# Second attention of a two-layer convolution/attention kernel: P*V by whole token halves, output rows begun with two quarters, the maximum of two quarters subtracted on TensorE, stores inside the written order

## The chip, the cores and the metric

One core of a Trainium2 chip runs the whole program. The metric is the device time of one execution in microseconds (us), lower is better. The engines are called PE (TensorE), DVE (VectorE), ACT (ScalarE), POOL (GpSimd) and SP (SyncE, which here only issues DMA transfers).

## The reference, cut to what matters

The input `x` is [1, 2048, 512]. Two layers follow each other, and both have a long convolution (part A) and a sliding attention with dilation (part B), each behind a layer norm and with a residual:

```
x = x + A(layernorm(x))     # y = irfft(rfft(K) * rfft(u)) + u * Dskip
x = x + B(layernorm(x))
x = x + A(layernorm(x))
x = x + B(layernorm(x))     # "the second attention": the part that is changed

def B(x):                   # 32 heads of 16; window of 8 keys, 2 apart
    q, k, v = split(x @ wqkv)
    logits[s, w] = q[s] . k[s - 2 w] / 4      (masked where s - 2 w < 0)
    attn = softmax(logits over w)
    o[s] = sum over w of attn[s, w] * v[s - 2 w]
    return o @ wo
```

## The kernel before

The 2,048 tokens lie as 16 rows `j` of 128 tokens; four rows form a group `X0` to `X3` (`Xg`). The 512 features are worked in four quarters `i` of 128 (8 heads each), the 16 rows in two token halves `jh` of 8 rows. For each quarter and half, `b_layer` does the following steps.

- `K` and `Q` (`proj`, L1170, L1173): PE projects, ACT copies out of PSUM. `V` (`proj_v`, L1257, L1264), then `M` (`v_shift`, L1281): DMAs on SP and POOL copy shifted rows of the value table.
- `L` (`logits`, L1218/L1220 and L1242): DVE multiplies queries with shifted keys, PE sums over the features of a head, ACT copies the logits to `Lsb`.
- `S` (`softmax`): DVE takes the maximum (L1301, L1307, L1309, with one PE exchange between the two lane halves). Then either DVE subtracts it in place (L1312) and ACT takes the exponent (L1313), which is what the second attention does; or, with `pe_max`, PE subtracts it in PSUM by two 512-column matmuls (L1319, L1320) and ACT takes the exponent from there (L1322), which is what the first attention does. PE sums the exponents (L1327), ACT takes the reciprocal (L1329, L1330), DVE multiplies (L1331).
- `P` (`pv_part`): DVE multiplies probabilities with shifted values (L1352), PE folds the products (L1362), ACT copies them out to `oT` (L1373). A part covers `nj` rows, 8 or 4, by the table `pv`. With 8 rows, one DVE instruction of 128x2048 does both lane halves of a key pair; with 4 rows two of 128x512 are issued.
- `R` (`out_row`): one output row `j`, 128 tokens by 512. PE adds up the residual (identity matmul, L1387) and four terms, one for each quarter of `oT` (L1389, the last one L1392 in rows of `early` and `early_l`). ACT or DVE copies the row out (L1406, L1404). For rows in `added`, the identity matmul is left out and DVE adds the residual as it copies (L1408). A row in `early` or `early_l` is begun when three quarters are there, and its last term is a step of its own.

The steps of one attention are put in order by a string that is written out in the source (`order` in `LAYERS`): every word is one step, `S31j` for instance step `j` of the softmax of quarter 3, half 1, and a `+` behind a word picks the second of its possible engines. Each engine runs its steps in the order of that string. The class `Plan` checks the order and keeps a running time from its own table of costs, from which alone it decides how many filler matmuls on zeros `stream` puts in PE's gaps (L1085); `keep=(share, columns)` says how much of a gap may be filled and how many columns are wanted in 3.41 us. In the order, `P28` is the part of quarter 2 from row 8, `P2c` that from row 12; rows 8 to f are hexadecimal.

After the last step, `store_x` issues seven stores: group 0 whole, group 1 whole, the rows of group 2 singly, group 3 whole, alternately on SP and on ACT:

```
for g in range(NG):
    n = 1 if g in LATE_GROUPS else 4
    for k in range(0, 4, n):
        (nc.sync if (g + k) % 2 == 0 else nc.scalar).dma_start(ov[...], Xg[g][:, k:k + n, :])
```

Of the kernel before, what the change touches and what calls it, by code (L numbers as in the profile page):

```python
# [11 lines left out]
ACT = mybir.ActivationFunctionType  # L12
# [8 lines left out]
D = 512  # L21
# [123 lines left out]


def store_x(nc, Xg, out2d):
    ov = out2d.rearrange("(p j) d -> p j d", j=NJ)
    for g in range(NG):
        n = 1 if g in LATE_GROUPS else 4  # L150
        for k in range(0, 4, n):
            (nc.sync if (g + k) % 2 == 0 else nc.scalar).dma_start(ov[:, g * 4 + k:g * 4 + k + n, :], Xg[g][:, k:k + n, :])
# [699 lines left out]
class Plan:  # L852
# [44 lines left out]
    def run(self, order):  # L897
# [16 lines left out]
        if todo:  # L914
# [9 lines left out]
LATE_GROUPS = (2,)  # L924
# [33 lines left out]
         pe_max=True,  # L958
# [3 lines left out]
         keep=(0.7, 4500),  # L962
# [4 lines left out]
         whole=()),  # L967
    dict(order="y0a y0b n0a n0b n0c y0c y0d n0d n0e n0i n0h y1a y1b y1c y1d n0f n1a n1c n0g n1b n1e n1d y2a n0j y2b y2c y3a n2a n0k n0l n1i n1g "
# [22 lines left out]
               "P3cj Reb Rcb R8a Rdb Rec Rcc+ Raa Rbb Rdc Rfa Rfb R8b Rab R9b",  # L991
         pv=[[8, 8], [8, 8], [8, 4], [8, 4]],
         soft=[0, 0, 0, 0],
         pe_max=False,
         early=[6, 12],
         early_l=[1, 4, 13, 14],
# [616 lines left out]
```

## Time and profile before

| | us |
|---|---|
| median of 3 runs | 438.28 (436.13 to 438.46) |
| profiled execution | 439.68 |
| span in its profile | 437.9 |
| DVE busy in the span | 402.4 (92%) |
| PE busy in the span | 379.9 (87%) |
| ACT busy in the span | 329.6 (75%) |
| mean granted TensorE clock | 0.977 |

The first attention runs from about 160 to 280 us, the second from about 320 us to the end. Busy shares are means over stages with different limits, so each stage has to be read by itself. Matmuls are pipelined: a row of several of them lasts longer than their number times the pitch between two starts.

### The profile page before, as it was taken

The numbers are of one execution on the slowest core, as the hardware profiler recorded it, in microseconds if no ns is written. First come the engines' busy times: TensorE is split into PE (matmuls) and PEld (weight loads), VectorE is DVE, ScalarE is ACT, GpSimd is POOL, SyncE is SP. The second block draws the span as 40 slices with busy tenths as digits, with TensorE's granted clock in tenths as the row PEclk, the third lists the DMA queues.
The fourth block names the chain that finished last, engine by engine and source line by source line (L and its number), as shares of the span: only waits on it lengthen the run. The fifth ranks groups of instructions, "written<-read, shape, count | busy, mean of one in ns | idle before, by whom it ended". The sixth has DMA issues, their size and how long they took to land.

```text
span 437.9 us, 12189 instructions
## 1 busy us (share of the span) xinstructions
PE 379.9 (87%) x5045; PEld 259.3 (59%) x5084; DVE 402.4 (92%) x783; ACT 329.6 (75%) x604; POOL 25.5 (6%) x66
## 2 busy tenths in 40 slices
PE   1176799999989989999997899789899999996995
PEld 1032586676468745686685465367746578784562
DVE  6999989999889969799999999999789999999993
ACT  6999979998989979755665399979969666652442
POOL 5000002001210000020010000000000002020000
PEclk9998779999999999999999899999999999999998
DMA  7900001254889930016043007458100003562022
GB/s 237 419 10 0 1 3 44 74 168 115 250 241 274 297 117 4 1 31 140 3 89 82 0 4 217 168 153 277 57 0 3 1 1 62 110 115 56 1 98 98
DMA packets 25647, 44.06 MB, mean 101 GB/s; under 512 B 7285, under 2 KB 17206, under 8 KB 24950
## 3 DMA queue, kind: packets, MB, share of 16 engines
q1 hardware_dynamic: 22630, 37.30, 29.4%
q0 software_dynamic: 1856, 4.53, 4.4%
q10 hardware_dynamic: 1104, 1.44, 0.9%
q8 instruction: 40, 0.66, 0.7%
q14 instruction: 17, 0.14, 0.1%
HBM read 29.01 MB, written 6.95 MB: 82 GB/s over the span
## 4 chain that ended last, share of the span: by engine, by line
PE 44%; DVE 21%; ACT 21%; issue 7%; DMA 6%; SPq 0%; POOL 0%; DVEq 0%; ACTq 0%; POOLq 0%
PE ps_qk L1170 10%; DVE prodpv L1352 7%; PE ps_v L1257 5%; PE psk L561 4%; DVE prodqk L1220 3%; PE Lp L1242 3%; PE psg L594 3%; ACT xc L272 3%; ACT Z L1426 3%; DVE Z L497 2%; PE pt L254 2%; PE vp L290 2%; PE xp L266 2%; DMA V<-V 2%; ACT X L1406 2%
## 5 line engine op out<-in xcount | busy, mean ns | idle before, releaser
L1352 DVE TENSOR_TENSOR prodpv<-V,Lsb 128x512 bf16<-128x512 bf16 (+1 forms) x124 | 79.4, 701 | 1.2 <-PE po L1362 1.1
L1170 PE MATMUL ps_qk<-xnT,wqk 128*128 128x512 bf16 x256 | 60.3, 379 | 0.0
L1362 PE MATMUL po<-halves,prodpv 128*128 128x64 bf16 x1024 | 38.9, 193 | 7.4 <-DVE prodpv L1352 5.8
L1218 DVE TENSOR_TENSOR prodqk<-qT,N 128x1024 bf16<-128x1024 bf16 (+3 forms) x88 | 42.5, 539 | 2.6 <-ACT N L1173 2.2
L1362 PEld LDWEIGHTS <-prodpv 128*128 128x128 bf16 x1024 | 34.8, 98 | 16.5 <-DVE prodpv L1352 11.1
L279 DVE TENSOR_TENSOR pab<-xc,Kt 128x2048 bf16<-128x2048 bf16 (+1 forms) x34 | 39.2, 1160 | 2.9 <-ACT xc L272 2.8
L1220 DVE TENSOR_TENSOR prodqk<-qT,N 128x512 bf16<-128x512 bf16 (+3 forms) x56 | 40.6, 762 | 0.7 <-ACT N L1173 0.6
L1373 ACT CAST oT<-po 128x512 bf16<-128x512 f32 x32 | 18.3, 595 | 27.4 <-PE po L1362 27.4
L1170 PEld LDWEIGHTS <-wqk 128*128 128x128 bf16 x256 | 23.9, 97 | 23.8
L272 ACT CAST xc<-xp 128x1024 bf16<-128x1024 f32 (+1 forms) x34 | 34.3, 1020 | 4.1 <-PE pt L254 2.8
L299 ACT CAST VT<-vp 128x1024 bf16<-128x1024 f32 (+1 forms) x32 | 33.2, 1052 | 3.1 <-PE vp L290 3.1
L290 PE MATMUL vp<-sb_IC,pab 128*128 128x128 bf16 x512 | 33.8, 219 | 1.2 <-ACT VT L299 0.4
L290 PEld LDWEIGHTS <-pab 128*128 128x128 bf16 x512 | 30.6, 98 | 6.0 <-issue 1.9
L1242 PEld LDWEIGHTS <-prodqk 128*128 128x128 bf16 x1024 | 29.6, 96 | 4.1 <-DVE prodqk L1218 0.6
L1242 PE MATMUL Lp<-sb_bones,prodqk 128*128 128x8 bf16 x1024 | 30.5, 166 | 0.2 <-DVE prodqk L1220 0.2
L1257 PE MATMUL ps_v<-wv,xnT 128*128 128x256 bf16 x256 | 30.4, 272 | 0.0
L521 PE MATMUL psadd<-Z,sb_ident 128*128 128x512 bf16 (+3 forms) x49 | 17.8, 376 | 12.6 <-DVE Z L497 8.2
L1389 PE MATMUL ps_o<-wo_t,oT 128*128 128x512 bf16 x91 | 26.4, 396 | 0.8 <-issue 0.2
L1257 PEld LDWEIGHTS <-xnT 128*128 128x128 bf16 x256 | 24.3, 97 | 3.6
L1173 ACT CAST qT<-ps_qk 128x512 bf16<-128x512 f32 x32 | 18.8, 593 | 7.5 <-PE ps_qk L1170 7.5
L1123 DVE BATCH_NORM_STATS2 ln_stats<-X 128x6 f32<-128x512 bf16 x37 | 23.7, 675 | 0.8 <-ACT X L1447 0.8
L1281 POOL DMA_DIRECT2D V<-V x16 | 8.9, 561 | 255.8 <-ACT V L1264 228.4
(201 smaller groups left out, 854.1 us busy)
## 6 DMA issues: line engine op xcount, KB each, us to landing
Kt<-kt_scratch SPq DMA_DIRECT2D x60, 256.0 KB
kt_scratch<-ks SPq DMA_DIRECT2D x32, 128.0 KB
G<-c_G SPq DMA_DIRECT2D x2, 1536.0 KB
V<-V SPq DMA_DIRECT2D x8, 288.0 KB
X<-in_A_u_dram SPq DMA_DIRECT2D x4, 512.0 KB
F1Tsb<-c_F1T SPq DMA_DIRECT2D x2, 1024.0 KB
V<-V SPq DMA_DIRECT2D x4, 512.0 KB
V<-V POOLq DMA_DIRECT2D x4, 384.0 KB, 7.3
```

Source lines behind the costliest of these rows:

```text
L272: nc.scalar.copy(xc[:, gs].rearrange("q g o l -> q (g o l)"), xp[:].rearrange("q h n -> q (h n)")[:, gs.start * 128:gs.stop * 128])
L279: nc.vector.tensor_tensor(pab[:, gs], xc[:, gs].to_broadcast([128, n, 2, 128]), kt[:, gs], ALU.mult)
L290: nc.tensor.matmul(vp[:, g, :], pab[:, g, ab, :], C["IC"][:, ab, :], start=(ab == 0), stop=(ab == 1))
L299: nc.scalar.copy(dst[..., gs], src[..., gs])
L1170: nc.tensor.matmul(t.ps[:], wqk[:, ct, f0:f0 + 128], x_group(g)[:, :, ct], start=(ct == 0), stop=(ct == 3))
L1218: nc.vector.tensor_tensor(b.pr[:, u:u + 2 * n, 1 - halves_of[0], :], q, cols(kT[i][:, starts[0]:starts[0] + n * 128]), ALU.mult)
L1220: nc.vector.tensor_tensor(b.pr[:, u:u + 2 * n].rearrange("f u a q -> f a u q")[:, ::-1], q.unsqueeze(1).to_broadcast([128, 2, 2 * n, 64]), ...
L1242: nc.tensor.matmul(t.Lp[:, w, u % 2, u // 2, :], b.pr[:, u].rearrange("f a q -> f (a q)"), bones[:], start=False, stop=(t.parts == W // 2 ...
L1257: nc.tensor.matmul(t.ps[:, jj, :], tokens(ct, jp * 2 + jj, c), wv[:, ct, fp * 256:(fp + 1) * 256], start=(jj + ct == 0), stop=(jj == 1 and ...
L1352: nc.vector.tensor_tensor(t.p2[:, c:c + k, 0:nj, :].rearrange("p c j (d h) -> p c j d h", d=DH), m.V2[i // 2][:, c0 + c:c0 + c + k, r0:r0 ...
L1362: nc.tensor.matmul(po[jj // k][:, jj % k, c, :], t.p2[:, c - c0, jj, :], fold, start=(first and c == c0 and jj % k == 0), stop=(last and c ...
L1389: nc.tensor.matmul(t["ps"][:], m.oT[:, ft, j * 128:(j + 1) * 128], wo_t[:, ft, :], start=(added and ft == 0), stop=False)
```

## The change

In the table of the second attention: all P*V parts cover 8 rows (`pv`), so that quarters 2 and 3 have no parts of 4 rows any more. `pe_max` becomes a list of quarters: PE subtracts the maximum in quarters 2 and 3, DVE still does so in quarters 0 and 1. The rows begun early are 10 to 15 (before 1, 4, 6, 12, 13, 14), and they are begun with two quarters; the third and the fourth term are steps of their own. DVE adds the residual in rows 8 and 9 only (before in 8 to 11). Eight stores are steps `O` of the order and are issued where it says, on SP or ACT: rows 0-3, 4-7, 8, 9, 10-11, 12-13, 14, 15. `store_x` is gone. The whole order of the second attention is another one. `keep` rises in both attentions; in the first attention nothing else changes. The options `kept` and `thirds` are empty for it.

```
-def store_x(nc, Xg, out2d):
...
     dict(order=  # first attention: the same order
-         pe_max=True,
+         pe_max=(0, 1, 2, 3),
-         keep=(0.7, 4500),
+         keep=(0.85, 6000),
...
     dict(order=  # second attention
...
-"... Q21a K12a K12b Q21b L100a L103a "
-"L102a t3d K13a K13b Q13a Q12a L101a L103c L102c L101b L100b L103b L101c Q00a Q13b Q12b L100c K02a L110a ..."
+"... K11b n3p t2d t2a Q01a t3a t3c t2b K12a Q01b t3b Q12a K12b L100a "
+"L101a L102a t3d L102c L103c K13a Q12b K13b Q13a Q00a L100b L100c K03a Q13b Q00b L103b L101b ..."
...
-"... P28h P28a P28f ... P38a P38d P38f P38b P28i P38c Rda P38g P38e P38h P3ca P3ch P3cf P38i Rea P3cd P28j R7b P3cb P38j Rba P3ci P3cc P3cg P3ce R9a Xa "
-"P3cj Reb Rcb R8a Rdb Rec Rcc+ Raa Rbb Rdc Rfa Rfb R8b Rab R9b",
-         pv=[[8, 8], [8, 8], [8, 4], [8, 4]],
+"... Rba P28c S31e P28g P28e P28i P28d O0b P28h S31f R4b S31g S31h S31i Rca P28f P28j Rda P28l P28k S31j P38a P38e P38i Rea Raa Rdb "
+"P38b Rfa P38c Rbb P38d P38j P38f P38g P38h Xa Rcb Reb Rfb Rab P38l P38k Rcc Rec Rcd+ Rac Rfc Rfd Rbc Rdc Red+ Rdd Rbd+ Rad Oca+ "
+"R9a R9b Oea+ Oaa+ Oab O9a+ O9b O4a Ofa O4b Oeb Ofb Ocb R8a R8b O8a+ O8b",
+         pv=[[8, 8], [8, 8], [8, 8], [8, 8]],
-         pe_max=False,
-         early=[6, 12],
-         early_l=[1, 4, 13, 14],
-         added=[8, 9, 10, 11],
-         keep=(0.5, 4500),
+         pe_max=(2, 3),
+         early=[12, 13, 14, 15],
+         early_l=[10, 11],
+         added=[8, 9],
+         keep=(0.85, 6000),
+         thirds=[12, 13, 14, 15, 10, 11],
+         stores=[(0, 4), (4, 4), (8, 1), (9, 1), (10, 2), (12, 2), (14, 1), (15, 1)]))
...
-            if not lay["pe_max"]:
+            if i not in lay["pe_max"]:
...
-            for k in range(n if lay["pe_max"] else 0):
+            for k in range(n if i in lay["pe_max"] else 0):
...
+            elif early:
+                n = 2 if j in lay["thirds"] else 3
+                alloc = p = plan.add("PE", 0.2165 * (n + (not added)), lambda: first(n), [o for i in range(n) for o in rows[i]], take=PL if in_l else PA)
+                for k in range(n, 4):
+                    p = plan.add("PE", 0.22, lambda k=k: terms(k, k + 1), [p] + rows[k])
...
+        def store(j0, n):
+            def move(eng):
+                (nc.sync if eng == "SP" else nc.scalar).dma_start(C["out"][:, j0:j0 + n, :], Xg[j0 // 4][:, j0 % 4:j0 % 4 + n, :])
+            o = plan.add(dict(SP=0.65, ACT=0.36), None, move, [got["X", j] for j in range(j0, j0 + n)])
+            plan.add("-", STORE_US + 0.32 * n, lambda: None, [o])
+        for j0, n in lay["stores"]:
+            part(f"O{j0:x}", store, j0, n)
...
-    store_x(nc, Xg, out[0])
```

More of the change, by code (lines that the diff above doesn't have):

```diff
@@ L921 @@
 V_LAND = 2.0
-LATE_GROUPS = (2,)
+STORE_US = 1.7
 LAYERS = (
@@ L966 @@
          joined=(2, 3),
-         whole=()),
-    dict(order="y0a y0b n0a n0b n0c y0c y0d n0d n0e n0i n0h y1a y1b y1c y1d n0f n1a n1c n0g n1b n1e n1d y2a n0j y2b y2c y3a n2a n0k n0l n1i n1g "
[22 rows of a table removed]
-               "P3cj Reb Rcb R8a Rdb Rec Rcc+ Raa Rbb Rdc Rfa Rfb R8b Rab R9b",
-         pv=[[8, 8], [8, 8], [8, 4], [8, 4]],
-         soft=[0, 0, 0, 0],
-         pe_max=False,
-         early=[6, 12],
-         early_l=[1, 4, 13, 14],
-         added=[8, 9, 10, 11],
-         keep=(0.5, 4500),
+         whole=(),
+         kept=[],
+         thirds=[],
+         stores=[]),
+    dict(order="y0a y0b n0a n0b n0c y0c y0d n0d y1a y1b n1a n0e n0g n0f n0i n1b n0h n1c y1c y1d n1e n1d y2a n0j y2b n2a y2c y3a n0k n1f n1h n0l "
[21 rows of a table added]
+               "P38b Rfa P38c Rbb P38d P38j P38f P38g P38h Xa Rcb Reb Rfb Rab P38l P38k Rcc Rec Rcd+ Rac Rfc Rfd Rbc Rdc Red+ Rdd Rbd+ Rad Oca+ "
+               "R9a R9b Oea+ Oaa+ Oab O9a+ O9b O4a Ofa O4b Oeb Ofb Ocb R8a R8b O8a+ O8b",
+         pv=[[8, 8], [8, 8], [8, 8], [8, 8]],
+         soft=[0, 0, 0, 0],
+         pe_max=(2, 3),
[3 more added lines that the diff above has]
+         keep=(0.85, 6000),
          y_sums=[[], [], [], []],
@@ L1381, in out_row, with tile_of, terms @@
             in_l = j in lay["early_l"]
-            def first():
+            kept = j in lay["kept"]
+            def tile_of():
                 t["ps"] = (m.psL if in_l else psA).tile([128, D], F32, name="ps_o", tag="psL" if in_l else "psA")
                 stream(t["ps"][:], True)
+            def terms(lo, hi, start=False):
+                for ft in range(lo, hi):
+                    nc.tensor.matmul(t["ps"][:], m.oT[:, ft, j * 128:(j + 1) * 128], wo_t[:, ft, :], start=(start and ft == lo), stop=(ft == 3 or kept and ft == 2))
@@ L1386, in first @@
+            def first(n=3):
+                tile_of()
                 if not added:
                     nc.tensor.matmul(t["ps"][:], ident[:], Xg[j // 4][:, j % 4, :], start=True, stop=False)
-                for ft in range(3):
-                    nc.tensor.matmul(t["ps"][:], m.oT[:, ft, j * 128:(j + 1) * 128], wo_t[:, ft, :], start=(added and ft == 0), stop=False)
-            def final():
-                nc.tensor.matmul(t["ps"][:], m.oT[:, 3, j * 128:(j + 1) * 128], wo_t[:, 3, :], start=False, stop=True)
@@ L1393, in out_row @@
-            if early:
-                alloc = plan.add("PE", 0.865, first, [o for i in range(3) for o in got["oT", i, j]], take=PL if in_l else PA)
-                p = plan.add("PE", 0.22, final, [alloc] + got["oT", 3, j])
+                terms(0, n, added)
+            rows = [got["oT", i, j] for i in range(4)]
+            if kept:
+                k = lay["kept"].index(j)
+                p = plan.add("PE", 0.865, first, rows[0] + rows[1] + rows[2] + [x_end], take=PA)
+                put = plan.add(dict(ACT=act_us(512), DVE=0.61), None, lambda eng: (nc.scalar.copy if eng == "ACT" else nc.vector.tensor_copy)(m.kept[:, k], t["ps"][:]), [p], drop=[p])
+                alloc = p = plan.add("PE", 0.22, lambda: (tile_of(), terms(3, 4, True)), [put] + rows[3], take=PL if in_l else PA)
+            elif early:
[3 more added lines that the diff above has]
+                    p = plan.add("PE", 0.22, lambda k=k: terms(k, k + 1), [p] + rows[k])
@@ L1396, in out_row @@
             else:
-                alloc = p = plan.add("PE", 0.865 if added else 1.08, lambda: (first(), final()), [o for i in range(4) for o in got["oT", i, j]], take=PA)
+                alloc = p = plan.add("PE", 0.865 if added else 1.08, lambda: (first(), terms(3, 4)), [o for i in range(4) for o in rows[i]], take=PA)
             x = Xg[j // 4][:, j % 4, :]
@@ L1406, in evict @@
                     nc.scalar.activation(x, t["ps"][:], ACT.Identity, **kw)
-            if added:
-                plan.add("DVE", 0.65, lambda: nc.vector.tensor_tensor(x, t["ps"][:], x, ALU.add), [p], drop=[alloc])
+            if added or kept:
+                got["X", j] = plan.add("DVE", 0.65, lambda: nc.vector.tensor_tensor(x, t["ps"][:], m.kept[:, k] if kept else x, ALU.add), [p], drop=[alloc])
                 return
             if last_layer:
-                plan.add(dict(ACT=act_us(512), DVE=0.61), None, evict, [p], drop=[alloc])
+                got["X", j] = plan.add(dict(ACT=act_us(512), DVE=0.61), None, evict, [p], drop=[alloc])
                 return
@@ L1521 @@
     prm = dict(A_re=A_A_re, A_im=A_A_im, B_re=A_B_re, B_im=A_B_im, C_re=A_C_re, C_im=A_C_im, log_dt=A_log_dt)
+    C["out"] = out[0].rearrange("(p j) d -> p j d", j=NJ)
     Xg = []
```

10 lines of the change are left out of this document (4 added, 6 removed), and 43 rows, old and new, of tables (stores, whole).

## The prediction

> **What bounds the kernel now.** I read the page first, for the engine that is fullest, and then the windows of the second attention, since all but a filler setting lies there. The windows give busy us by engine for PE, PEld, DVE, ACT and POOL, then the granted clock and the DMA share.
>
> ```profile
> span 437.9 us, 12189 instructions
> ...
> PE 379.9 (87%) x5045; PEld 259.3 (59%) x5084; DVE 402.4 (92%) x783; ACT 329.6 (75%) x604; POOL 25.5 (6%) x66
> ```
>
> ```profile
> 340.00:345.00 5.00, 5.00 (x25) 2.28 (x24) 4.21 (x10) 3.76 (x7) 0.00 (x0) 1.00 0.00 0
> ...
> 385.00:390.00 5.00, 5.00 (x140) 4.42 (x139) 5.00 (x7) 2.18 (x5) 2.22 (x4) 1.00 0.52 112
> 390.00:395.00 5.00, 4.12 (x95) 3.15 (x92) 5.00 (x11) 3.42 (x8) 0.00 (x0) 1.00 1.02 170
> 395.00:400.00 5.00, 3.44 (x70) 2.28 (x68) 5.00 (x7) 1.71 (x6) 0.00 (x0) 1.00 0.44 89
> 400.00:405.00 5.00, 3.27 (x68) 2.35 (x70) 5.00 (x5) 0.48 (x2) 0.00 (x0) 1.00 0.01 3
> 405.00:410.00 5.00, 4.17 (x87) 2.94 (x85) 5.00 (x7) 1.05 (x3) 0.00 (x0) 1.00 0.00 0
> ...
> 425.00:428.20 3.20, 3.17 (x56) 2.11 (x54) 3.14 (x10) 0.58 (x1) 0.00 (x0) 1.00 0.41 164
> 428.20:433.50 5.30, 4.55 (x29) 1.92 (x25) 3.17 (x5) 2.38 (x4) 0.00 (x0) 1.00 0.19 63
> 433.50:437.90 4.40, 0.00 (x0) 0.00 (x0) 0.00 (x0) 0.00 (x0) 0.00 (x0) 0.70 0.45 168
> ```
>
> Three stretches follow each other. Until 428 us DVE works without a pause (one gap of 0.8 us, below); PE is as full as DVE up to about 390 us and has room behind that. From 428.2 to 433.5 us a chain from the last product through PE, ACT and DVE leads to the last store. From 433.5 us no engine works: 4.4 us of transfer and completion. So the change is priced in three pieces: DVE work taken away, length of the closing chain, length of the last transfer.
>
> **Term 1, the DVE's work.** The timeline rows below give start, length and count of runs of DVE instructions; the group gives the length of one.
>
> ```profile
> 393.86 4.62 DVE L1352 TENSOR_TENSOR prodpv<-V,Lsb 128x2048 bf16<-128x2048 bf16 x4
> ...
> 418.06 0.41 DVE L1312 TENSOR_TENSOR Lsb<-Lsb,sm_mx 128x512 bf16<-128x512 bf16 x1
> 418.40 3.22 DVE L1352 TENSOR_TENSOR prodpv<-V,Lsb 128x2048 bf16<-128x2048 bf16 x7
> ...
> 422.02 6.12 DVE L1352 TENSOR_TENSOR prodpv<-V,Lsb 128x512 bf16<-128x512 bf16 x18
> 429.82 0.69 DVE L1404 CAST X<-ps_o 128x512 bf16<-128x512 f32 x1 [1.68 <-PE ps_o L1392]
> 430.43 2.62 DVE L1408 TENSOR_TENSOR X<-ps_o,X 128x512 bf16<-128x512 f32 x4
> ```
>
> ```profile
> L1352 DVE TENSOR_TENSOR prodpv<-V,Lsb 128x2048 bf16<-128x2048 bf16 x24 | 28.3, 1216 | 0.0
> ...
> L1352 DVE TENSOR_TENSOR prodpv<-V,Lsb 128x512 bf16<-128x512 bf16 x32 | 11.0, 415 | 0.0
> ```
>
> Neighbouring instructions overlap, so what counts is the pitch. Four products of 2048 take 4.62 us with a last one of 1.22: (4.62 - 1.22) / 3 = 1.135 us. Eighteen of 512 take 6.12: (6.12 - 0.415) / 17 = 0.336 us. The change turns the 32 small ones into 8 large ones: 32 x 0.336 - 8 x 1.135 = 10.75 - 9.08 = 1.67 us less. The subtraction of a maximum takes 418.40 - 418.06 = 0.34 us of DVE; in two quarters with two halves each, four of them go: 1.36 us. Both sums are ahead of the last product, in the stretch that DVE bounds: 3.0 us together. Two adds turn into two copies on DVE; the copy takes 430.43 - 429.82 = 0.61, an add (2.62 - 0.69) / 3 = 0.64, so this is nothing, and it lies behind the last product.
>
> **What DVE loses again.** One wait interrupts it near the start of the attention:
>
> ```profile
> 342.34 3.18 DVE L1218 TENSOR_TENSOR prodqk<-qT,N 128x1024 bf16<-128x1024 bf16 x6 [0.79 <-ACT N L1173]
> ```
>
> This is the logits products waiting for keys that ACT still copies out. In the order before, `L102c` stands behind `K13a K13b Q13a Q12a` and three products of other keys. In the new order it comes straight after `t3d`, five words behind `K12b`, the copy that brings its keys, and `L100b` three words behind `K13b`, on which it hangs in the same way. So there are two such waits where there was one. I give back 1.0 us: one wait of 0.8 and 0.2 for smaller ones. The bounds are 0 (other products cover them) and 2.0 (two waits more, and the rest of PE's work below).
>
> **PE's side of it.** PE gets eight matmuls of 512 columns for the four subtractions, and two identity matmuls, since rows 10 and 11 get their residual on PE now. The filler of the second attention, counted in the built programs, falls from 3,072 to 1,088 columns.
>
> ```profile
> 425.86 1.46 PE L1389 MATMUL ps_o<-wo_t,oT 128*128 128x512 bf16 x6
> ...
> 427.37 1.12 PE L1362 MATMUL po<-halves,prodpv 128*128 128x64 bf16 x32
> 428.53 0.58 ACT L1373 CAST oT<-po 128x512 bf16<-128x512 f32 x1 [2.10 <-PE po L1362]
> ```
>
> The pitch of a 512-column matmul is (1.46 - 0.38) / 5 = 0.216 us, 0.38 being the length of one. Ten of them are 2.2 us, and 1,984 columns of filler are 0.84 less. Between 395 and 410 us PE is idle for 1.56 + 1.73 + 0.83 = 4.1 us, which is the cover, and I take 0 beyond what is given back above. If that cover is gone, because the new order fills the same gaps with the row terms it begins early, it costs up to 2.2 us (first rival). The Trainium skill, "TensorE: Matmul & The Clock Gate", section "Back-to-back issue gap", has 131 ns for each 512-column matmul in a sustained stream; by that the ten would cost 1.3 us. The 0.216 us of the row decides here.
>
> So the last product should end 3.0 - 1.0 = 2.0 us earlier, near 426.1 instead of 428.1 us (422.02 + 6.12). Between the bounds it is 1.0 to 3.0 us.
>
> **Term 2, the closing chain.** Before, it runs from 428.1 us to the last store, at 433.5 us (the second of the two issues in the row below; the copy ahead of it ends at 433.44): 5.4 us.
>
> ```profile
> 432.84 0.60 ACT L1406 ACTIVATE X<-ps_o 128x512 bf16<-128x512 f32 x1 [1.35 <-DMA out_dram<-X]
> 433.08 0.86 ACTq L152 DMA_DIRECT2D out_dram<-X  x2
> ```
>
> The new chain: folding 16 products, half of the 32 in 1.12 us with the end of a matmul, 0.65; one copy to `oT` 0.58; the fourth term of six rows, 6 x 0.216 = 1.30; rows 9 and 8 whole, with four terms each, 8 x 0.216 = 1.73, and 0.16 until the last one is through; the add 0.69; four handovers of some 0.05, 0.2. The sum is 5.3 us. The second copy to `oT`, the copies of rows and the other issues lie beside it. Five issues now stand at the end of ACT's queue, each behind a wait for a copy or an add; what is queued behind a waiting one is only the next store. At 0.43 us each (0.86 for two) the four ahead of the last need 1.7 us, about what PE takes for rows 9 and 8, so that they may hold the last one up a little. I take 0.1 us longer than before: 0 to +0.5.
>
> **Term 3, the last transfer.** Before, the last store is a group of 512 KB.
>
> ```profile
> 432.00:433.00 1.00, 0.81 (x4) 0.19 (x2) 1.00 (x2) 0.16 (x1) 0.00 (x0) 1.00 0.75 251
> ...
> 434.50:435.00 0.50, 0.00 (x0) 0.00 (x0) 0.00 (x0) 0.00 (x0) 0.00 (x0) 1.00 1.00 393
> ...
> 436.00:437.90 1.90, 0.00 (x0) 0.00 (x0) 0.00 (x0) 0.00 (x0) 0.00 (x0) 0.50 0.01 4
> ```
>
> Its data have flowed by 436.0 us, 2.5 us behind the issue, and 1.9 us go by until the end. After, the last store has one row, 128 KB. At 393 GB/s the 393 kB fewer are 1.0 us. But one-row stores flow at 251 GB/s (the first row above), and rows 8 to 15, 1.05 MB, are issued only once the fourth terms are through, 1.73 + 0.16 + 0.69 = 2.6 us ahead of the last issue. At 251 GB/s they need 4.2 us. The 512 KB store took 2.5 us, 1.3 of them at 393 GB/s, which leaves 1.2 us for its start; so the data would end -2.6 + 1.2 + 4.2 = 2.8 us behind the last issue, 0.3 later than before. Between a loss of 0.3 and a gain of 1.0 I take a gain of 0.6, since four of the eight rows go in pairs, which are nearer to the large stores.
>
> **The sum.** -2.0 + 0.1 - 0.6 = -2.5 us: span 437.9 to 435.4, and the profiled time 439.68 (1.78 us lie outside the span) to 437.2. The profiled execution is 1.4 us above the median, 438.28; the difference taken from the median gives **435.8 us**. The terms' bounds give -0.2 (-1.0 + 0.5 + 0.3) to -4.0 (-3.0 + 0 - 1.0).
>
> **Rivals.**
> *PE takes it back.* The rows' early terms fill the gaps that I use as cover, and PE bounds the stage behind 400 us. For it: PE is at 5.00 of 5 up to 390 us already, so any gap that closes makes both engines full. Against it: 4.1 us of room, and the filler shrinks. Price: 2.2 us, so -0.3: 438.0 us.
>
> *The clock falls in the second attention* (the one that ends on the other side). In the first attention it happens:
>
> ```profile
> 240.00:244.00 4.00, 2.65 (x61) 2.16 (x61) 4.00 (x11) 1.07 (x2) 0.00 (x0) 1.00 0.00 0
> 244.00:248.00 4.00, 3.78 (x14) 1.57 (x16) 4.00 (x7) 0.58 (x1) 0.00 (x0) 0.57 0.00 0
> ...
> 251.50 0.76 DVE L1352 TENSOR_TENSOR prodpv<-V,Lsb 128x512 bf16<-128x512 bf16 x2 [1.07 <-PE po L1362]
> ```
>
> After 4 us with PE busy for 2.65, the clock is 0.57 in the next four; (1 - 0.57) x 4 = 1.7 us of PE work is lost, and soon DVE waits 1.07 us for PE. In the second attention the clock stays at 1.00 with PE busy 3.44 and 3.27 of 5, partly with filler. Two thirds of the filler go. Should the clock fall there, PE has much to do right behind it, and each such stretch costs 1.7 us; from two on the gain is gone: -2.5 + 3.4 = +0.9, 439.2 us. With three it is 440.9. Against it: the early row terms and the subtractions put real work where the filler was. The Trainium skill, "TensorE: Matmul & The Clock Gate", section "What's actually happening", has the clock halve after one or more idle windows of 3.4 us that run freely; by that rule one execution may fall and the next not. The trace agrees in the length, but PE was not idle before it, only two thirds busy.
>
> *The fall in the first attention goes away.* There filler rises from 384 to 640 columns, 256 x 0.216 / 512 = 0.1 us of work, part of it in those 4 us. If that is enough, the 1.07 us of waiting are saved too: -3.6, 434.7 us. Against it: 0.1 us in 4 is little.
>
> **How the numbers follow.** A measurement of this kernel can tell about 0.5%, 2.2 us, from no change: faster is below 436.1, slower above 440.5 us. The forecast has 0.56; being 0.3 us from that bound, 0.36 of it counts as faster and 0.20 as same. PE taking it back has 0.18: 0.17 same and 0.01 slower. The clock falling has 0.10, half same and half slower. The first attention's fall going away has 0.16, all faster. That makes 0.52, 0.42 and 0.06. The range runs from 433.9 (the last rival with 0.8 us more from terms 1 and 3) to 438.3, which takes in the forecast's weak end (438.1) and PE's case, and leaves out the clock falling twice.
>
> **What would show it.** Right, step by step: no 128x512 product in the second attention and 32 of 128x2048; four subtractions on DVE; DVE full up to a last product near 426; about 5.5 us from there to the last issue; under 4.1 us from it to the end. Wrong: waits of DVE for PE between 400 and 426 us (PE takes it back), a clock below 1.00 between 390 and 430 us (the second rival), or a last transfer as long as before.

## The result, and the profile after

| | before | after |
|---|---|---|
| median of 9 runs, us | 438.46 (436.13 to 439.73) | 434.89 (433.30 to 435.98) |
| profiled execution, us | 439.68 | 435.94 |
| span in its profile, us | 437.9 | 434.2 |
| mean granted TensorE clock | 0.977 | 0.980 |

The changed kernel takes 0.9927 of the time before, with a 95% interval of 0.9908 to 0.9945: it is faster by 0.73%, and the medians differ by 3.6 us where 2.5 were forecast. The page of the changed kernel, span and totals by engine:

```profile
span 434.2 us, 12182 instructions
...
PE 378.6 (87%) x5056; PEld 260.5 (60%) x5094; DVE 400.0 (92%) x755; ACT 331.0 (76%) x604; POOL 25.3 (6%) x66
```

DVE has 2.4 us less to do in 28 instructions fewer, PE 1.3 us less; the span is 3.7 us shorter. To see where, the span is cut at one instruction that both programs have: the copy to `VT`, the last step of the convolution that comes before the second attention. The DVE timelines of before and after (start, length, and in brackets the idle time and what ended it):

```profile
319.13 0.69 DVE L297 CAST VT<-vp 128x512 bf16<-128x512 f32 x1 [2.51 <-ACT VT L299]
```

```profile
318.78 0.69 DVE L289 CAST VT<-vp 128x512 bf16<-128x512 f32 x1 [2.51 <-ACT VT L291]
```

From there to the end it is 437.9 - 319.13 = 118.77 us before and 434.2 - 318.78 = 115.42 after. So 3.35 us come from the changed stage, and 0.35 from what lies ahead of it. The rest of this document compares this length, "the stage", because the part ahead of it scatters by several us from one execution to the next, as the experiments show. The stage is steadier, but it is not exact. Two programs that leave the changed kernel's stage as it is (e5 and e7) have it within 0.04 and 0.34 us of after; the latter comes from one pause of 0.3 us on DVE for which the profile names no cause. With the old order and the old stores, the time behind the last row is 4.5 us in one profile (before) and 4.1 in another (e8). So a difference of less than about 0.4 us between two stages is not told from none.

**The DVE's part.** The windows from the copy to the end of the last product, first before, then after (busy us for PE, PEld, DVE, ACT, POOL, then clock, DMA share, GB/s):

```profile
319.13:428.14 109.01, 102.77 (x1495) 70.12 (x1503) 107.84 (x226) 65.05 (x126) 4.46 (x8) 1.00 0.21 45
```

```profile
318.78:425.68 106.90, 102.62 (x1495) 70.77 (x1501) 105.25 (x198) 66.41 (x125) 4.43 (x8) 1.00 0.20 46
```

The last product is 2.11 us nearer to the copy. DVE's busy time falls by 2.59 us, its idle time rises by 0.48 (1.17 to 1.65). The groups after and the list of DVE's waits (waited for: total, times, longest) say what changed:

```profile
L1352 DVE TENSOR_TENSOR prodpv<-V,Lsb 128x2048 bf16<-128x2048 bf16 x32 | 37.7, 1220 | 0.0
...
L1312 DVE TENSOR_TENSOR Lsb<-Lsb,sm_mx 128x512 bf16<-128x512 bf16 x4 | 1.7, 420 | 0.0
```

```profile
DVE prodqk L1218 <- ACT N L1173: 1.0, 2, 0.6
DVE prodqk L1220 <- ACT qT L1173: 0.2, 1, 0.2
```

The 128x512 products are gone, four of eight subtractions are left on DVE, and the waits at the logits products are 1.2 us in three places instead of 0.8 in one. DVE waits nowhere for PE ahead of its last product, though PE did take more of its own gaps:

```profile
395.00:400.00 5.00, 3.63 (x93) 3.11 (x93) 5.00 (x9) 2.38 (x6) 0.00 (x0) 1.00 0.02 3
400.00:405.00 5.00, 4.56 (x77) 2.97 (x75) 5.00 (x6) 1.31 (x4) 0.00 (x0) 1.00 0.02 3
405.00:410.00 5.00, 4.88 (x87) 3.32 (x86) 5.00 (x6) 2.13 (x5) 0.00 (x0) 1.00 0.00 0
```

PE's idle time in these 15 us is 1.37 + 0.44 + 0.12 = 1.93 us, where it was 4.12. So 2.19 us of the cover are used up, and DVE stays at 5.00 of 5 all the same. The clock is at 1.00. What uses them is above all the row terms begun early. PE's groups of term matmuls in these 15 us, before and after:

```profile
L1389 PE MATMUL ps_o<-wo_t,oT 128*128 128x512 bf16 x6 | 1.8, 381 | 0.1
```

```profile
L1391 PE MATMUL ps_o<-wo_t,oT 128*128 128x512 bf16 x18 | 4.7, 379 | 0.1
```

Of the four subtractions on PE, only one lies here, near 397 us; the others are near 386, 394 and 418 us.

**The end.** The timeline of the changed kernel from its last products on (`ACTq` is the queue that issues the stores):

```profile
423.32 2.35 DVE L1352 TENSOR_TENSOR prodpv<-V,Lsb 128x2048 bf16<-128x2048 bf16 x2
...
424.23 2.14 PE L1362 MATMUL po<-halves,prodpv 128*128 128x64 bf16 x64
...
426.43 3.88 PE L1391 MATMUL ps_o<-wo_t,oT 128*128 128x512 bf16 x17
...
429.30 2.38 ACTq L1508 DMA_DIRECT2D out_dram<-X  x5
...
430.34 0.69 DVE L1421 TENSOR_TENSOR X<-ps_o,X 128x512 bf16<-128x512 f32 x1 [0.17 <-PE ps_o L1391]
```

From the end of the last product, 425.68, to the last store's issue, near 431.3, it is 5.6 us (5.4 before). The last row is complete at 431.03, and the span ends 3.2 us later; before, the last row's copy ended at 433.44, and it took 4.5 us. The windows show the bytes:

```profile
429.50:430.00 0.50, 0.50 (x4) 0.19 (x2) 0.50 (x1) 0.26 (x1) 0.00 (x0) 1.00 0.69 229
430.00:430.50 0.50, 0.31 (x2) 0.00 (x0) 0.33 (x2) 0.00 (x0) 0.00 (x0) 1.00 0.77 270
430.50:431.00 0.50, 0.00 (x0) 0.00 (x0) 0.50 (x1) 0.00 (x0) 0.00 (x0) 1.00 1.00 359
...
431.50:432.00 0.50, 0.00 (x0) 0.00 (x0) 0.00 (x0) 0.00 (x0) 0.00 (x0) 1.00 1.01 373
...
432.50:433.00 0.50, 0.00 (x0) 0.00 (x0) 0.00 (x0) 0.00 (x0) 0.00 (x0) 1.00 0.48 158
```

Rows 8 to 15, 1.05 MB, flow between 429.5 and about 432.75 us, and the rate climbs to 373 GB/s once several stores are under way. At 251 GB/s, the rate that the prediction took for single rows, they would have needed a microsecond more.

### The profile page after: what moved, and what is told of

It reads as the page before. It is cut to its first block, busy times and chain, and to the rows that moved or that the text cites. A ratio compares the mean times of both kernels' runs of the same rounds, so it can differ in the third digit from the quotient of the medians.

```text
span 434.2 us, 12182 instructions
## 1 busy us (share of the span) xinstructions
PE 378.6 (87%) x5056; PEld 260.5 (60%) x5094; DVE 400.0 (92%) x755; ACT 331.0 (76%) x604; POOL 25.3 (6%) x66
## 3 DMA queue, kind: packets, MB, share of 16 engines
q10 hardware_dynamic: 1248, 1.05, 0.7%
## 4 chain that ended last, share of the span: by engine, by line
PE 39%; DVE 26%; ACT 20%; issue 7%; DMA 6%; SPq 1%; DVEq 0%; POOLq 0%; ACTq 0%
DVE prodpv L1352 10%; PE ps_qk L1170 8%; DVE prodqk L1220 5%; PE psk L553 4%; PE psg L586 3%; ACT xc L264 3%; DVE Z L489 3%; ACT Z L1439 3%; PE ps_o L1391 3%; PE pt L246 2%; DMA V<-V 2%; PE vp L282 2%; PE xp L258 2%; PE ps_v L1257 2%; PE Lp L1242 2%
## 5 line engine op out<-in xcount | busy, mean ns | idle before, releaser
L1352 DVE TENSOR_TENSOR prodpv<-V,Lsb 128x2048 bf16<-128x2048 bf16 (+1 forms) x100 | 77.9, 836 | 1.4 <-PE po L1362 1.3
L1391 PE MATMUL ps_o<-wo_t,oT 128*128 128x512 bf16 x123 | 33.1, 387 | 0.8 <-issue 0.2
L513 PE MATMUL psadd<-Z,sb_ident 128*128 128x512 bf16 (+3 forms) x49 | 16.7, 354 | 12.9 <-DVE Z L489 8.2
L1264 ACT CAST V<-ps_v 128x512 bf16<-128x512 f32 x32 | 18.1, 588 | 9.5 <-PE ps_v L1257 9.5
```

The costliest lines, as they stand in the source:

```text
L1352: nc.vector.tensor_tensor(t.p2[:, c:c + k, 0:nj, :].rearrange("p c j (d h) -> p c j d h", d=DH), m.V2[i // 2][:, c0 + c:c0 + c + k, r0:r0 ...
L1391: nc.tensor.matmul(t["ps"][:], m.oT[:, ft, j * 128:(j + 1) * 128], wo_t[:, ft, :], start=(start and ft == lo), stop=(ft == 3 or kept and f ...
```

## The experiments

All of them are variants of the changed kernel, unless "before" is said. The table has the median of the timed runs, the ratio to runs of the kernel before on the same chip, and three lengths from the one profile that each program has: when the first attention begins (the first `ln_stats`), how long it lasts (to the first transposition behind it), and the stage, from the copy to `VT` to the end. What lies between the first attention and that copy took 35.5 us in each of them. The runs were made in three sets, e1 to e4, e5 to e8 and e9 to e12; beside them the kernel before had medians of 437.41, 438.66 and 438.09 us, so that medians are compared within a set, and ratios between sets.

| | median, us | ratio (95%) | begins | first attention | the stage |
|---|---|---|---|---|---|
| before | 438.46 | 1 | 158.86 | 124.77 | 118.77 |
| after | 434.89 | 0.9927 (0.9908-0.9945) | 158.31 | 124.97 | 115.42 |
| e1, DVE subtracts | 441.87 | 1.0099 (1.0069-1.0129) | 157.93 | 123.27 | 123.21 |
| e2, small products | 435.85 | 0.9957 (0.9933-0.9980) | 159.20 | 124.79 | 116.72 |
| e3, old stores | 435.27 | 0.9951 (0.9926-0.9975) | 156.82 | 123.09 | 116.09 |
| e4, three quarters | 437.48 | 0.9986 (0.9964-1.0008) | 157.81 | 123.36 | 117.94 |
| e5, after again | 435.57 | 0.9929 (0.9901-0.9957) | 158.07 | 124.96 | 115.38 |
| e6, little filler | 433.73 | 0.9890 (0.9870-0.9911) | 157.12 | 124.72 | 115.36 |
| e7, first attention filled | 433.58 | 0.9891 (0.9874-0.9908) | 156.87 | 123.17 | 115.76 |
| e8, before + PE subtracts | 436.68 | 0.9959 (0.9942-0.9975) | 157.04 | 123.08 | 118.58 |
| e9, e1 + filler | 441.25 | 1.0070 (1.0049-1.0091) | 157.54 | 124.81 | 122.76 |
| e10, before + single stores | 437.60 | 0.9999 (0.9976-1.0022) | 157.24 | 124.56 | 118.60 |
| e11, other order of stores | 435.04 | 0.9931 (0.9917-0.9946) | 157.97 | 124.89 | 115.45 |
| e12, e7 and e11 | 433.50 | 0.9898 (0.9880-0.9916) | 157.99 | 123.09 | 115.43 |

The first attention comes in two lengths, 123.1 to 123.4 and 124.6 to 125.0 us, whatever was done to the second. That is 1.7 us of scatter between executions of any of these kernels; the beginning adds up to 2.4. This is why effects under 2 us are read from the stage.

### e1: DVE subtracts the maximum in all quarters

```
-         pe_max=(2, 3),
+         pe_max=(),
```

> The changed kernel, but DVE subtracts the maximum in quarters 2 and 3 again (four instructions of 0.34 us), and the eight matmuls on PE are gone. Theory (DVE sets the pace up to the last product): 1.36 us longer than the changed kernel, between 1.0 and 1.4. Rival (PE sets the pace from 400 us on, where its windows show 4.6 to 4.9 of 5 us): no longer at all, or up to 0.5 us shorter, since PE loses 1.7 us of work.

Neither expectation holds: the stage grows by 7.8 us and the kernel is slower than the one before. DVE's timeline, PE's waits, and windows of 2 us:

```profile
393.66 1.21 DVE L1352 TENSOR_TENSOR prodpv<-V,Lsb 128x2048 bf16<-128x2048 bf16 x1
394.80 0.41 DVE L1312 TENSOR_TENSOR Lsb<-Lsb,sm_mx 128x512 bf16<-128x512 bf16 x1
397.21 0.42 DVE L1331 TENSOR_TENSOR Lsb<-Lsb,sm_rdb 128x512 bf16<-128x512 bf16 x1 [2.00 <-ACT sm_rdb L1330]
```

```profile
PE den L1327 <- ACT Lsb L1313: 8.5, 2, 4.5
```

```profile
398.00:400.00 2.00, 2.00 (x40) 1.98 (x38) 2.00 (x2) 0.00 (x0) 0.00 (x0) 0.50 0.00 0
...
402.00:404.00 2.00, 0.00 (x0) 0.00 (x0) 1.84 (x3) 0.13 (x1) 0.00 (x0) 0.50 0.00 0
```

In DVE's queue the subtraction now stands behind a product of 1.2 us. ACT's exponent hangs on it, and PE's sum of the exponents (L1327) hangs on that. PE's next work is queued behind this sum: PE stands still for 4.5 and 4.0 us, and DVE in its turn waits for the reciprocal (2.0) and for the folds of its products (2.9 in two waits). The clock falls to 0.50 from 395 to 408 us as well. Which of the two made the loss, the waiting or the clock, e9 decides.

### e2: the last eight large products as 32 small ones

```
-  nc.vector.tensor_tensor(t.p2[:, c:c + k, 0:nj, :]...)        # 128x2048
+  for h in range(0, nj, 4):                                    # quarters 2, 3 from row 8
+      nc.vector.tensor_tensor(t.p2[:, c, h:h + 4, :]...)       # 128x512
```

> The changed kernel with the same parts and order, but the products of the second token half of quarters 2 and 3 issued as 32 instructions of 128x512 in place of 8 of 128x2048. Theory (DVE sets the pace): 1.67 us longer (32 x 0.336 - 8 x 1.135). Rival (PE sets the pace there): under 0.8 us longer.

```profile
422.57 5.45 DVE L1355 TENSOR_TENSOR prodpv<-V,Lsb 128x512 bf16<-128x512 bf16 x16
```

The stage is 1.30 us longer. The last product ends at 422.57 + 5.45 = 428.02, 108.54 us behind the copy to `VT`, which is 1.64 later than after, against the 1.67 of the working. The chain behind it is 0.3 shorter: PE begins the closing row terms 0.4 us behind the last product, where it was 0.75 in the changed kernel, which has larger products left to fold there. So the size of the products is worth 1.64 us in the place where the prediction put it, and 1.3 at the end.

### e3: the stores after the last step, as before

```
-         stores=[(0, 4), (4, 4), (8, 1), (9, 1), (10, 2), (12, 2), (14, 1), (15, 1)]))
+         stores=[]))          # and no O words in the order
...
+    store_x(nc, Xg, out[0])   # groups 0, 1, 3 whole, rows 8 to 11 singly
```

> The changed kernel without the store steps in its order; the seven stores of the kernel before stand at the end, so that rows 12 to 15 go as one store of 512 KB. Theory (what follows the last issue is shorter because the last pieces are small): about 1.0 us longer, 0.6 to 1.5. Rival (only the time at which the last row is ready counts, the bytes flow at the same rate either way): within 0.3 us of the changed kernel.

The stage is 0.67 us longer: the first expectation's case, at its lower end, and not the rival's. Its last add, and a window of 0.5 us behind it:

```profile
427.14 0.69 DVE L1407 TENSOR_TENSOR X<-ps_o,X 128x512 bf16<-128x512 f32 x1 [0.17 <-PE ps_o L1377]
```

```profile
428.50:429.00 0.50, 0.00 (x0) 0.00 (x0) 0.00 (x0) 0.00 (x0) 0.00 (x0) 1.00 1.06 418
```

Its data start later and flow faster, at up to 418 GB/s: the last row is complete at 427.83, and from there it takes 431.5 - 427.83 = 3.7 us to the end. With the new stores it is 3.1 to 3.2 us in all ten profiles that have them; with the old order and the old stores it is 4.5 (before) or 4.1 (e8). So the new order with the old stores has 0.4 to 0.8 of the gain behind the last row already, and the new stores add 0.5.

### e4: rows 10 to 15 begun with three quarters

```
-  alloc = p = plan.add("PE", 0.2165 * (n + (not added)), lambda: first(n), ...)
+  alloc = p = plan.add("PE", 0.2165 * (n + (not added)), lambda: None if late else first(n), ...)
...
-      p = plan.add("PE", 0.22, lambda k=k: terms(k, k + 1), [p] + rows[k])
+      p = plan.add("PE", 0.22, lambda k=k: first(3) if late and k == 2 else terms(k, k + 1), [p] + rows[k])
```

> The changed kernel, but the six rows begun early are begun only when the third quarter is there, at the place in the order where their third term stood. Four of those places are behind the fold of the last products, so 4 x 3 = 12 matmuls of 0.216 us come into the closing chain, less about 0.9 us in which PE waits there for the copies to oT. Theory (PE bounds the closing chain): 1.7 us longer, 1.2 to 2.6. Rival (the chain hangs on ACT's and DVE's copies): under 0.6 us longer.

The stage grows by 2.5 us, within the first expectation and past the rival's. DVE's wait for the first row to copy out:

```profile
DVE X L1418 <- PE ps_o L1391: 4.4, 1, 4.4
```

It was 1.8 us in the changed kernel. The early row terms, which cost nothing in PE's gaps, are 2.6 us of PE work on the closing chain when they come with the third quarter; the 0.9 us of waiting that was to cover a part of them is not seen. The 2.5 us are no gain against the kernel before, which began six rows with three quarters each (1, 4, 6 and 12 to 14) in an order of its own; they say what the early terms are worth in the new one.

### e5, e6: the changed kernel once more (no edit), and with little filler (e6's edit)

```
-  keep=(0.85, 6000),      # first attention       +  keep=(0.7, 4500),
-  keep=(0.85, 6000),      # second attention      +  keep=(0.5, 4500),
```

> The changed kernel as it is, on the same chip as the next three, as their base. From the last step of the convolution on DVE (the copy to VT, at 318.8 us in the changed kernel's profile and 319.1 in the one before) to the end of the span it should take 115.4 us again, within 0.3, whatever the opening takes.

> The changed kernel with the old filler settings, (0.7, 4500) and (0.5, 4500). With the new order that leaves no filler at all in the second attention, and 384 columns in the first. Theory (the subtractions and the early row terms keep PE busy enough): clock at 1.00 from 390 us on, and the same time within 0.5 us. Rival (the clock is held only by the filler): the clock falls to 0.5 between 390 and 410 us, 1.7 us longer for each 3.4 us of it.

e5 repeats the stage to 0.04 us. In e6 the second attention has no filler at all. Windows of 10 us in it:

```profile
390.00:400.00 10.00, 7.17 (x133) 4.90 (x131) 10.00 (x16) 4.95 (x11) 0.00 (x0) 1.00 0.01 2
400.00:410.00 10.00, 9.25 (x125) 5.82 (x128) 10.00 (x12) 4.88 (x10) 0.00 (x0) 1.00 0.01 2
```

The clock is granted in full with PE 72% and 93% busy, and the stage is as long as after: here the row terms and subtractions suffice. So the raised `keep` is worth nothing in the stage. The median is 1.8 us below e5's, outside the 0.5 that were expected, and nothing in the stage accounts for it. Its profiled execution begins the first attention 0.95 us earlier than e5's and has a long first attention too. Whether the scatter ahead of the stage falls otherwise in this program, or more runs would level it, stays open.

### e7: filler in the first attention, where its clock falls

```
+  if not last_layer and i == 2 and j0 == 0:     # before the folds of quarter 2, first half
+      plan.fill = 2048 if first else 1024       # 5,120 columns of zeros in all
```

> The changed kernel with 5,120 columns of filler forced into the four folds of quarter 2, first half, in the first attention, ahead of the stretch where the clock falls in the changed kernel's profile (240 to 247 us) and where DVE then waits 1.28 us for PE. Theory (that fall costs what DVE waits): no fall there, 0.6 to 1.3 us shorter in the median than the changed kernel, since not every execution has the fall. Rival (the fall hangs on the phase of the clock's windows, not on this work, or the filler delays PE as much): within 0.3 us.

Windows of 4 us in the first attention, after and then e7:

```profile
240.00:244.00 4.00, 3.20 (x56) 2.93 (x53) 4.00 (x12) 1.07 (x2) 0.00 (x0) 0.50 0.00 0
244.00:248.00 4.00, 3.78 (x19) 1.69 (x18) 4.00 (x8) 0.58 (x1) 0.00 (x0) 0.66 0.00 0
```

```profile
236.00:240.00 4.00, 3.77 (x70) 2.29 (x71) 4.00 (x6) 0.05 (x2) 0.00 (x0) 1.00 0.02 4
240.00:244.00 4.00, 3.34 (x44) 2.05 (x43) 4.00 (x11) 1.62 (x3) 0.00 (x0) 1.00 0.00 0
244.00:248.00 4.00, 4.00 (x38) 2.11 (x37) 4.00 (x9) 2.25 (x7) 0.00 (x0) 1.00 0.02 4
```

There is no fall, DVE does not wait for PE there (1.3 us before the edit), and the first attention takes 123.17 us. One profile doesn't show that the filler did it, for e3, e4 and e8 have no fall without it. The runs speak for it: the mean clock of all five is 0.986 to 0.992, where e5's six have 0.973 to 0.988, and e12 below has the filler and no fall either. The median is 2.0 us below e5's, more than the 0.6 to 1.3 that were expected. It can't be put to the filler alone, for e6 has nearly the same median without it, and with a fall in its profile.

### e8: the kernel before, with PE's subtraction alone

```
-         pe_max=False,
+         pe_max=(2, 3),
```

> The kernel before with one part of the change alone: PE subtracts the maximum in quarters 2 and 3 of the second attention, in the old order. Theory (DVE sets the pace, and four subtractions of 0.34 us leave it): 1.36 us shorter than the kernel before, between 0.8 and 1.4. Rival (PE, at 5.00 of 5 us up to 390 us, pays 1.7 us for it in the same stretch): within 0.4 us, or longer.

The stage is shorter by 0.19 us, not by 1.36, and even this is no gain of DVE's. The last products:

```profile
418.72 6.12 DVE L1352 TENSOR_TENSOR prodpv<-V,Lsb 128x512 bf16<-128x512 bf16 x18
```

They end at 424.84, 109.22 us behind the copy to `VT`; before it was 109.01. The last row is 0.2 us later as well. What is shorter is the time behind it, 4.1 us where before has 4.5, with the same order and the same stores. DVE's waits in the stage that the kernel before doesn't have:

```profile
DVE prodqk L1220 <- PE Lp L1242: 0.7, 1, 0.7
DVE Lsb L1331 <- ACT sm_rdb L1330: 0.4, 1, 0.4
DVE prodqk L1220 <- ACT N L1173: 0.3, 1, 0.3
```

These 1.3 us give the DVE work back. It is the size that the rival named; half of it is a wait for PE, as the rival has it, and half are waits for ACT. The medians differ by 2.0 us; in the profiled execution the difference lies ahead of the stage (beginning 1.8 earlier, first attention 1.7 shorter), where the two programs compute the same. It is no effect of the edit that these runs show.

The end of this program's transfer shows what scatters there. Windows of 0.5 us of it, for the span that ends at 434.2:

```profile
432.00:432.50 0.50, 0.00 (x0) 0.00 (x0) 0.00 (x0) 0.00 (x0) 0.00 (x0) 1.00 0.86 344
432.50:433.00 0.50, 0.00 (x0) 0.00 (x0) 0.00 (x0) 0.00 (x0) 0.00 (x0) 1.00 0.01 0
```

The data end at 432.5 us, 1.7 us ahead of the end of the span. In the profile of before a trickle of 16 GB/s still flows between 436.0 and 436.5 us, and from there it is 1.4 us to the end.

### e9: e1 with filler ahead of the sums

```
-         pe_max=(2, 3),
+         pe_max=(),
...
+  plan.fill = {(3, 0): 14 * 512, (2, 1): 10 * 512}.get((i, a), 0) if last_layer else 0
+  stream(t.den[:], True)          # 7,168 and 5,120 columns ahead of PE's two late sums
```

> The first experiment again (DVE subtracts in quarters 2 and 3), with filler on zeros in PE's queue ahead of the sums of exponents of quarter 3, first half (7,168 columns), and quarter 2, second half (5,120 columns), where PE stood idle for 4.05 and 4.47 us. Theory (without PE's subtractions the clock falls, and that is most of the 7.8 us which the second attention lost): clock 1.00 up to the last product; from the VT copy to the end 118.5 us, between 117.5 and 119: 115.4, four subtractions of 0.34, and the wait of some 1.7 us that DVE has for its own subtraction's way through ACT and PE and back. Rival (the waiting itself is the loss, the clock only its sign): 121 us or more.

```profile
402.00:404.00 2.00, 0.00 (x0) 0.00 (x0) 2.00 (x3) 0.00 (x0) 0.00 (x0) 1.00 0.00 0
```

With the clock at 1.00 but for 3.4 us near 408, the stage is 122.76 us, only 0.45 less than in e1: not the 118.5 that the theory has, but the rival's case. DVE's waits that the changed kernel doesn't have:

```profile
DVE prodpv L1354 <- PE po L1364: 2.7, 2, 1.7
...
DVE Lsb L1333 <- ACT sm_rdb L1332: 1.8, 1, 1.8
DVE sm_m L1301 <- ACT Lsb L1245: 1.1, 1, 1.1
```

They are 5.6 us, and four subtractions of 0.34 are 1.4: 7.0 of the 7.3 us above the changed kernel. So the waiting is the loss, and the clock hardly matters. In the new order PE's subtraction is not a saving that could be left out: it takes this step of the softmax out of DVE's queue, where it would stand behind a product. That order was written with PE's subtraction in it; what another order could do with DVE's was not tried.

### e10: the kernel before, with four single stores for the last group

```
-LATE_GROUPS = (2,)
+LATE_GROUPS = (2, 3)
```

> The kernel before, with the 512 KB store of rows 12 to 15 cut into four stores of one row. The order stays, so these rows are still the last to be ready and four issues follow them. Theory (two things shorten the last transfer in the change: smaller pieces, and rows 12 to 15 being ready ahead of rows 8 and 9): from the last copy of a row to the end 4.5 us before, 3.9 to 4.5 here, against 3.2 in the changed kernel. Rival (the size of the last store is all): 3.4 us or less. From the VT copy to the last product 109.0 us, as before, within 0.2.

```profile
431.00 0.60 ACT L1406 ACTIVATE X<-ps_o 128x512 bf16<-128x512 f32 x1 [0.57 <-PE ps_o L1392]
```

```profile
432.50:433.00 0.50, 0.00 (x0) 0.00 (x0) 0.00 (x0) 0.00 (x0) 0.00 (x0) 1.00 1.06 340
...
433.50:434.00 0.50, 0.00 (x0) 0.00 (x0) 0.00 (x0) 0.00 (x0) 0.00 (x0) 1.00 0.06 18
434.00:436.00 2.00, 0.00 (x0) 0.00 (x0) 0.00 (x0) 0.00 (x0) 0.00 (x0) 1.00 0.00 2
```

From the end of the last copy, 431.60, to the end of the span, 435.9, it is 4.3 us. That lies between the 4.5 of before and the 4.1 of e8, which have the old stores in this order, while after has 3.2. So smaller stores alone bring nothing here that can be told. The data have nearly all flowed by 433.5, yet a trickle goes on until past 434. The changed kernel's windows show none, and e8's neither. Why some executions have one is not settled.

This program also shows a fall of the clock in the second attention, 0.66 from 395 to 400 us, with DVE at 5.00 of 5 throughout and the last product 109.00 us behind the copy, as before (109.01).

### e11, e12: the last stores shared between SP and ACT; the same with e7's filler

```
-"... Rbd+ Rad Oca+ R9a R9b Oea+ Oaa+ Oab O9a+ O9b O4a Ofa O4b Oeb Ofb Ocb R8a R8b O8a+ O8b"
+"... Rbd+ Rad O4a Ofa Oea Oca Oaa+ R9a R9b O9a+ R8a R8b O8a O4b Ofb Oeb Ocb Oab O9b O8b"
```

> The changed kernel with its last six stores shared out otherwise: rows 14, 12-13 and 8 on SP, rows 10-11 and 9 on ACT, so that no issue waits behind four others. Theory (the closing transfer begins late because ACT issues five stores one after the other, 0.41 us each): from the VT copy to the end 0.3 to 0.5 us less than 115.4. Rival (the bytes bound it, 1.05 MB at 370 GB/s): within 0.15 us.

> The changed kernel with both the filler of the first attention and the stores shared out. If both hold: no fall of the clock in the first attention, 123.1 us there, and the median 1.5 to 2.3 us below the changed kernel's; if only the filler holds, 1.2 to 1.9.

e11's stage is 115.45 us: no gain, the rival's case. Its windows of 0.5 us:

```profile
429.00:429.50 0.50, 0.50 (x5) 0.19 (x2) 0.45 (x1) 0.33 (x1) 0.00 (x0) 1.00 0.56 186
...
432.00:432.50 0.50, 0.00 (x0) 0.00 (x0) 0.00 (x0) 0.00 (x0) 0.00 (x0) 1.00 0.77 254
```

The data start and end with the last row as they do in the changed kernel: from the last add to the end it is 3.2 us in both, though e11 issues its last store right behind that add, near 430.6, and the changed kernel 0.3 us behind it. So the issues are not what holds the end up, but the bytes. The Trainium skill, "DMA: Bandwidth & Descriptors", section "Issuing engines are not separate DMA queues", says that starting transfers from several engines saves only the time of issuing, as all run on the same 16 engines; the run agrees.

e12 takes 433.50 us, 0.9898 of the kernel before, with no fall in the first attention (123.09) and a stage of 115.43. With e7 it is the shortest version here, and the two don't differ measurably, so the order of the stores adds nothing. Against e11, which was run beside it and has the same stage, it is 1.5 us, 0.35%, less in the median, and five of its six runs have a mean clock of 0.986 or more, where e11's have 0.976 to 0.984. That the filler does this is likely, with e7 and e12 agreeing; e6, which is as short as e7 and has only 384 columns of filler in the first attention, keeps it from being shown.

## Why the prediction was right, and where it was off

The forecast was 435.8 us with a range of 433.9 to 438.3; 434.9 was measured. Against the profiled execution it said -2.5 us; the stage gave -3.35, and -0.35 came from what lies ahead of it.

**Term 1** was right in its sum: the last product was to come 2.0 us earlier, and came 2.11. That it is right to 0.1 is luck, for two errors of about 0.4 and 0.5 us cancel in it. The products are worth their 1.67 us (e2: 1.64 up to the last product). DVE's busy time fell by 2.59 us and not by 3.0; the give-back was taken as 1.0 us for a wait of 0.8 and some smaller ones, and DVE's idle time rose by 0.48, in waits of 0.56, 0.43 and 0.24 at the logits products. The first two are the ones that the prediction read out of the order, and together they are hardly longer than the one of 0.79 before. So the work saved was 0.4 too large and the give-back 0.5 too large. That the subtraction is worth its 1.36 us of DVE time can't be said of it by itself: in the old order it comes back as waits and the last product is no earlier (e8), and in the new order its absence costs 7.8 us (e1). It belongs to the order, and the prediction priced it as if it did not.

**PE's cover** held, with DVE never waiting for PE ahead of the last product, but it was used otherwise than the prediction has it. The 2.2 us of added work were expected to go into 4.1 us of idle time between 395 and 410 us. That 2.19 us of it are gone is a coincidence: one subtraction lies there, and the rest is mainly the early row terms, which are what the first rival feared. They came, and 1.93 us of idle time were still left. The pitch taken for them fits the last 17 row terms, (3.88 - 0.38) / 16 = 0.219 us; the 131 ns of the Trainium skill's "Back-to-back issue gap" ("TensorE: Matmul & The Clock Gate") are not reached here. So the first rival, that PE takes the gain back, is out in this kernel; e4 shows what the same row terms cost where no gap takes them, 2.5 us.

**Term 2**, the closing chain, was taken 0.1 us longer and is about 0.3 longer, within its bounds of 0 to 0.5.

**Term 3** is the term that was mis-sized: the last transfer was taken 0.6 us shorter, between a loss of 0.3 and a gain of 1.0, and from the last issue to the end it is 1.5 us shorter in these profiles (4.4 to 2.9), or 1.1 against e8, which has 4.0 with the old stores and order. Two steps of its working failed. The rate of single rows was read as 251 GB/s from a slice in which stores were being issued one by one; with several of them under way it climbs to 373, so the data end about 1.45 us behind the last issue and not 2.5 or more. And the time from the last data to the end, 1.9 us in the old profile, was carried over unchanged, while it is about 1.45. The row quoted for it before shows what went unread there: in its last 1.9 us a mean of 4 GB/s still flowed, the trickle up to 436.5, behind which it is 1.4 us there too. Of the gain behind the last complete row, 0.9 to 1.3 us, e3 puts 0.5 on the new stores and the rest on the new order, and e10 shows that the smaller stores alone, in the old order, bring nothing that can be told.

**The clock.** The second rival, a fall in the second attention, did not come in the changed kernel, not even with no filler at all (e6). Its price was wrong: each fall was to cost the 1.7 us of PE work that it takes away. In e10 one fell from 395 to 399 us and cost the DVE nothing; in e1 against e9 ten microseconds more of half clock cost 0.45 us. So a fall costs what then waits for PE, not what PE loses. In the first attention the long form is 1.7 us longer in before than in e8; 1.07 us of that are DVE's wait for PE, 0.33 a wait for ACT a little later, and the rest is not located. The third rival, that the fall in the first attention goes away, did not happen in the profiled execution: with 640 columns of filler instead of 384 the clock was still 0.50 from 240 to 244 us. With 5,120 columns in the right gaps it didn't come in either profile (e7, e12). Where the fall is absent, the first attention is 1.7 us shorter, and not the 1.07 of the one wait that the rival priced.

Of these falls the Trainium skill, "TensorE: Matmul & The Clock Gate", section "What's actually happening", says that the clock halves after one or more idle windows of 3.4 us, and that the windows run freely, so that equal executions may differ. The second half agrees: profiled executions with the first attention's code unchanged have the fall (of the old code before and e10, of the changed one after, e2, e5, e9 and e11) or don't (e8; e3 and e4), and in e1 it came near 238 us, six microseconds earlier than before, and no DVE wait followed. On the first half the measurement decides: PE was busy for 2.65 of the 4 us ahead of the fall in the kernel before, and for 1.78 of the 4 us ahead of those, so it doesn't take a window without work.

## What to carry to other kernels

Cut both spans at an instruction that the change doesn't touch and compare stage with stage: here the whole time scattered by over 4 us in one program, while the stage repeated to within 0.4. Price the end of a kernel from the bytes that are still to flow when the last row is complete and from the rate that they reach together, not from a slice in which stores come one at a time. An operation that moves between engines is worth what waits behind it in the queue that it leaves, and this depends on the order around it: the same subtraction was worth nothing in one order and 7.8 us in the other.

## What the runs showed of the hardware

- A longer time mostly goes with a lower mean granted clock, but not closely. Of the six runs of e5 the slowest had 437.26 us at a mean clock of 0.973 and the fastest 433.08 at 0.988. Of the nine of the changed kernel, the fastest (433.30) and the slowest (435.98) both had 0.980.
- The clock also falls in the opening part, and by differing amounts. Windows of the kernel before and of e3, where no attention has begun and both compute the same:

```profile
28.00:62.00 34.00, 26.57 (x292) 16.54 (x294) 33.00 (x62) 30.24 (x62) 0.32 (x1) 0.80 0.01 1
```

```profile
28.00:62.00 34.00, 26.23 (x377) 17.74 (x377) 33.87 (x64) 31.93 (x67) 0.31 (x1) 0.90 0.01 2
```

  The three profiles with 0.90 here (e3, e7, e8) begin the first attention at 156.8 to 157.0 us, those with 0.80 or 0.85 at 157.1 to 159.2.
- Filler of 5,120 columns, 2.2 us of PE work by the pitch of 0.216, went into the first attention without making it longer: it takes 123.17 us in e7 and 123.09 in e12, as in the executions without a fall (123.1 to 123.4).
